# A new hand-written order for four engines, and fewer normalisation shifts, in a fused linear-attention and gated-MLP kernel

## The chip, the cores and the metric

The kernel runs on one core of one Trainium2 chip. The metric is the device time of one execution in microseconds (us), the median of several runs. The core has five engines that run independently and each take their instructions strictly in order: TensorE (PE, matrix products; the profile lists its weight loads apart as PEld), VectorE (DVE), ScalarE (ACT), GpSimd (POOL) and SyncE (SP, which only issues loads and stores here). An instruction that needs a result of another engine waits on a semaphore, and everything behind it on its own engine waits with it.

## The reference, cut to what matters

Inputs: q, k, v, alpha of shape (4 batches, 8 heads, 768 steps, 48), w_in (384 x 1024), w_spatial (768 x 768), b_spatial (768), w_out (512 x 384).

```
state = alpha[t][:, None] * state + k[t] (x) v[t]     # per batch and head, a 48 x 48 state
y[t]  = q[t] @ state                                   # 768 steps; heads joined: x is (4, 768, 384)
h = relu(x @ w_in); u, v = h[..., :512], h[..., 512:]
v_n = (v - mean(v)) / sqrt(var(v) + 1e-6)              # over the 512 columns of a row
v_s = w_spatial @ v_n + b_spatial                      # mixes the 768 rows of a batch
out = (u * v_s) @ w_out
```

## The kernel before

**The work and its tiles.** A batch has six chunks of 128 steps, so there are 24 chunks, numbered i = 0 to 23 (j = i // 2 numbers pairs of chunks). The recurrence is done by chunks: logarithms of alpha are summed by matmuls, exponentials of the sums scale k and q (`kt`, `qt`), both are turned by TensorE (`tr`, `trk`) and copied back (`ev`, `evs`), scores k by q are taken (`sc`) and multiplied by a mask (`m`, `ms`), and `y` adds masked scores times v and q times the state so far. Between chunks the state is carried: `upd` (k by v), `z` (sum with the old state), `S` (scaled by the decay), `sb` (bf16 copy). `xe` copies y out as the transposed input of the MLP. Chunks 0 to 3 and 6 to 9 are taken four at a time (`four_chunks`), 4 and 5 as a pair, the others singly.

The MLP follows per batch b: `v` and `u` (products with the two halves of w_in), `ve` and `ue` (relu out of the bank), then the normalisation of a row tile: `bn` (two VectorE instructions, L1068 and L1069: statistics), `rs` (two ScalarE instructions for a pair of row tiles, L1078 and L1079: 1 / sqrt(var + eps) as exp(-0.5 ln)), `nm` (the shift -mean / sqrt, L1085) and `vn`, the normalised tile. Then `s` (spatial mixing, for four column blocks d and two halves th of the rows; in two parts, of which the second needs the row tiles 4 and 5), `se` (bias added), `g` (times u), `o` (product with w_out), `oe` (copy out) and `st` (store).

**Two ways to normalise.** `vn` exists for two engines. ScalarE computes scale * x + shift and so needs `nm`; VectorE computes (x - mean) * rstd from the mean itself and never reads the shift. In the kernel before, one `nm` operation makes both shifts of a pair of row tiles, on VectorE, whichever engine normalises them: 12 operations, 24 instructions. Both `vn` of the pair depend on it.

```
def vnf(e, x=x):
    if e == "ACT":
        nc.scalar.activation(
            out=vn[n2][:, x, :], in_=v_sb[n2][:, x, :], func=AF.Identity, bias=shift[n2][:, x:x + 1],
            scale=rstd[n2][:, x:x + 1])
        return
    nc.vector.tensor_scalar(
        out=vn[n2][:, x, :], in0=v_sb[n2][:, x, :], scalar1=mvs[n2][:, x, 0:1],
        scalar2=rstd[n2][:, x:x + 1], op0=ALU.subtract, op1=ALU.mult)
```

**What sets the order.** Functions such as `pair`, `project_v`, `mix` only list operations, each with a key, the engines that could do it, what it depends on and how many of the eight PSUM banks it takes. The order, the engine of each operation and its banks stand in the string `PLAN`, which `replay` (L110) walks through: `D79` is operation 79 on VectorE (P TensorE, A ScalarE, G GpSimd, S SyncE), `@4,5` are its banks. Each engine gets its operations in the order of the table. `:512#0` puts a filler ahead of the operation: a matmul of the constant tile `junk` with 512 columns in fp32 into bank 0 (L243), whose result nobody reads; one filler is two matmul instructions in the profile. Before, there are seven fillers: three of 512 columns ahead of the first matmul, 512 and 424 ahead of the first state update `upd`, one of 192 and one of 376 ahead of two operations behind it.

**Loads.** SyncE issues all loads of q, k, v, alpha and the weights in one fixed order. Weights arrive as fp32 in two raw buffers in turn and are cast to bf16 (`cast`): w_in's v half, w_in's u half, three thirds of w_spatial, w_out. A raw buffer is loaded again only when all casts out of it are done; so the second third of w_spatial waits for the three casts of w_in's u half, and the last third for the two casts of the first third. w_spatial is turned in six steps on TensorE (`wt`) and copied back (`we`).

**Orders that matter below** (key.batch-or-chunk.index). VectorE between the last `qt` of chunks 4 and 5 and the last `vn` of batch 0, before: ev.k.2, ev.q.2, bn.0.2, bn.0.0, four m.2, bn.0.3, z.4, bn.0.1, nm.0.2, we.1, we.0, nm.0.0, ve.0.4, we.0, we.2, vn.0.0, vn.0.1, we.2, vn.0.3, bn.0.4, bn.0.5, two qt (chunks 6 to 9), nm.0.4, ue.0.2, vn.0.4; ScalarE normalises vn.0.2 and vn.0.5. GpSimd casts all three tiles of w_in's u half, then two vb, S.3, sb.3, both casts of w_spatial's first third, S.4. Around chunk 10 VectorE does bn.1.0, the first masks of chunks 10 and 11, z.10, their second masks, bn.1.1, bn.1.2, ve.1.3, bn.1.3.

Of the kernel before, what the change touches and what calls it, by code (L numbers as in the profile page):

```python
# [37 lines left out]
LETTERS = {"P": "PE", "D": "DVE", "A": "ACT", "G": "POOL", "S": "SP"}  # L38
# [4 lines left out]
D2 D0 D4 D1 G9 G11 G5 G6 D3 S56 S57 S59 S58 A60 S12 S169 S170 A61 S272 S171 D8 P62@0:512#0:512#0:512#0 P66@1 P67 P63  # L43
P70@2 P71 P74@3 P75 A68 A64 D79 G82 P91@4,5 P52@6 A69 A72 A76 G7 A78 A92 A84 A65 G88 G87 A73 A77 D85 D90 D81 D93 D53
D83 D80 P103@6,4,5,7:512#7:424#7 P94@0,1 D86 D104 D89 D106 G13 P97@6,2:192#2 D98 A95 P100@3,0 D101 A96 P117@3,6:376#1
P115@4,1 A99 G107 G14 A15 A173 D102 D109 P128@0,2 D119 D118 P174@5 A116 A122 A176 P130@6,4 S16 D132 D131 S172 A135
P175@1 A129 P120@3 P54@2 G110 G105 P136@0,4 A121 A178 A55 G111 G108 P133@6 G181 A180 A134 G184 A179 D112 A177 D138
P123@7,3 P141@2 S20 G276 G277 G278 G17 G19 G18 D124 D125 P151@6 P187@7,4 P126@3 S23 S274 S273 D185 A152 A127 G186 G183
G113 G114 D182 P190@5,6 A189 A192 A142 P144@3 D137 P139@4 D188 D191 A140 G22 G21 D153 D143 P199@6,5 P196@2,7 P162@4
A280 A145 P287@0 A163 P154@1 P160@3 A279 A288 A155 D200 D201 D198 D197 D164 P193@4 A161 P156@7 A157 A165 D194 D146  # L50
P158@5 A159 G195 P202@1,2 P203 S26 A204 A147 D166 P290@4 P37@5,7 D38 P34@3,6 G24 S275 S384 S396 G25 S503 S29 D35
P207@1 D148 D208 D36 A39 A289 P205 P281@7 P40@3,5 A206 A282 A167 G10 D42 P210@2 D149 D150 D41 S385 S386 D168 D209 S398
S397 P284@5 P223@6 P219@3 P221@1 A211 A291 A224 A285 D212 A283 A220 A213 D295 D301 A286 A292 D214 D222 D215 A216
P225@6 P233@2 P217@3 P229@7 P237@0 A218 A28 D298 G297 G27 D304 G294 P226 D227 G300 G303 P43@3,5 D45 P230 P234 D231
D235 A293 A44 P46@4,6 P306@5,1 D308 P238 P49@7,3 D50 D51 A48 A47 A307 P309@2,6 P315@1,4 P312@5,7 P249@3 P250 A310 A316
# [52 lines left out]


def replay(ops, held, warm, plan):  # L110

    for word in plan.split():
        word, *junk = word.split(":")
        word, *banks = word.split("@")
        op, eng = ops[int(word[1:])], LETTERS[word[0]]
# [1160 lines left out]
```

## Time and profile before

| | |
|---|---|
| median of 3 runs | 138.26 us (138.02 to 138.45) |
| the profiled execution | 139.19 us |
| its span, first to last instruction | 137.4 us |
| granted TensorE clock | 1.00 |
| instructions | 5308 |
| read from HBM, written | 23.60 MB, 4.72 MB |

The profile is of one execution. Its span lies 1.8 us below that execution's time; the rest is start and end of the program. A line of the timeline holds the start and length in us, the engine, the line of the kernel, the operation, what it writes from what, its shape and how many neighbours are merged; behind it in brackets the idle time ahead of it and what ended that. A line of the groups ends with busy us, mean ns of one, and the idle time before. In the chain of waits each piece is what held up the end of the program at that time. In the lines of stretches the busy time of each engine stands with its number of instructions. Lines L181, L185, L187 and L190 are helpers (copy, relu on ScalarE, relu on VectorE, product), L1006 every long matmul: there the tile names tell what it is.

### The profile page before, as it was taken

The page shows a single profiled execution, that of the slowest core. Times are in us where ns is not written, and L with a number is a line of the kernel's source. Part 1 is how long each engine was busy: PE and PEld are TensorE (multiplying, and loading weights), DVE is VectorE, ACT ScalarE, POOL GpSimd, SP SyncE. Part 2 cuts the span into 40 slices and gives each one's busy share as a digit, 9 for nine tenths or more (in the row PEclk, how much of TensorE's full clock was granted, in tenths as well). Part 3 has the DMA queues.
Part 4 walks back from the last instruction along what each step waited for, and adds up shares of the span by engine and source line. Part 5 has one row for each costly group of instructions (what it writes and reads, how often), then busy time and mean ns, then how long its engine had stood idle before and what let it go on. Part 6 is the DMA issues. An engine that isn't in the chain of part 4 may idle for free.

```text
span 137.4 us, 5308 instructions
## 1 busy us (share of the span) xinstructions
PE 131.0 (95%) x2122; PEld 79.2 (58%) x2122; DVE 120.8 (88%) x300; ACT 108.0 (79%) x261; POOL 87.2 (63%) x146
## 2 busy tenths in 40 slices
PE   6899998999999999999999999999999999999990
PEld 3365554564646566566657666656566765565560
DVE  6259999979999999999899999997999999974871
ACT  3476998899989889999997989999965796954041
POOL 7365899967399789972079989620799842003560
PEclk9999999999999999999999999999999999999999
DMA  3999999599989796899999797899991497101055
GB/s 83 371 371 382 341 321 347 132 374 383 366 164 261 159 218 127 163 184 192 195 190 209 143 205 147 167 194 226 190 181 23 158 390 257 66 0 57 0 203 203
DMA packets 76473, 28.66 MB, mean 209 GB/s; under 512 B 63008, under 2 KB 74912, under 8 KB 76448
## 3 DMA queue, kind: packets, MB, share of 16 engines
q1 hardware_dynamic: 76416, 28.32, 78.6%
q8 instruction: 16, 0.26, 0.8%
q14 instruction: 9, 0.07, 0.2%
q0 software_dynamic: 32, 0.00, 0.0%
HBM read 23.60 MB, written 4.72 MB: 206 GB/s over the span
## 4 chain that ended last, share of the span: by engine, by line
PE 76%; ACT 6%; DVE 6%; DMA 5%; issue 3%; POOL 2%; SPq 0%; POOLq 0%; ACTq 0%
PE bank L1006 53%; DMA kc<-in_k_dram 5%; PE bank L961 3%; PE bank L945 3%; PE bank L989 3%; PE bank L417 2%; PE bank L855 2%; PE bank L899 2%; PE bank L837 2%; PE bank L933 2%; DVE vn L1097 1%; PE bank L795 1%; PE bank L772 1%; ACT uT L185 1%; DVE w_spT L181 1%
## 5 line engine op out<-in xcount | busy, mean ns | idle before, releaser
L1006 PE MATMUL bank<-w_spT,vn 128*128 128x384 bf16 x192 | 35.8, 327 | 0.3 <-DVE vn L1097 0.3
L190 POOL TENSOR_TENSOR gT<-vs,uT 128x384 bf16<-128x384 f32 x28 | 25.7, 933 | 14.3 <-DVE vs L1153 14.1
L190 POOL TENSOR_TENSOR kt<-kc,binv 128x384 bf16<-128x384 f32 x22 | 20.3, 931 | 20.3 <-ACT binv L909 15.2
L1006 PEld LDWEIGHTS <-vn 128*128 128x128 bf16 x192 | 17.4, 98 | 11.7 <-DVE vn L1097 0.7
L1006 PE MATMUL bank<-w_in,xT 128*128 128x512 bf16 x72 | 19.1, 380 | 0.2 <-ACT xT L179 0.2
L1006 PE MATMUL bank<-xT,w_in 128*128 128x384 bf16 x96 | 18.7, 326 | 0.0
L1006 PE MATMUL bank<-w_out_sb,gT 128*128 128x384 bf16 (+1 forms) x100 | 18.4, 320 | 0.0
L1153 DVE TENSOR_TENSOR vs<-bank,bsp_bc 128x384 f32<-128x384 f32 x31 | 16.3, 550 | 2.4 <-PE bank L1006 2.3
L950 DVE TENSOR_TENSOR ptm<-bank,mask 128x512 bf16<-128x512 f32 x28 | 17.9, 683 | 0.4 <-PE bank L945 0.2
L179 ACT COPY kqT<-bank 128x512 bf16<-128x512 bf16 (+1 forms) x20 | 15.0, 792 | 3.1 <-PE bank L989 1.9
L1068 DVE BATCH_NORM_STATS2 stats<-v_sb 128x6 f32<-128x512 bf16 x24 | 16.4, 682 | 0.2
L185 ACT ACTIVATE v_sb<-bank 128x512 bf16<-128x512 f32 x20 | 11.8, 599 | 1.8 <-PE bank L1006 1.5
L185 ACT ACTIVATE uT<-bank 128x384 bf16<-128x384 f32 x27 | 12.4, 495 | 0.7 <-PE bank L1006 0.6
L1006 PEld LDWEIGHTS <-w_in 128*128 128x128 bf16 x96 | 9.0, 98 | 6.7 <-DVE ptm L950 0.3
L190 DVE TENSOR_TENSOR qt<-qc,bank 128x384 bf16<-128x384 f32 x24 | 12.6, 545 | 0.2 <-DMA qc<-in_q_dram 0.2
L1006 PEld LDWEIGHTS <-gT 128*128 128x128 bf16 x100 | 9.3, 98 | 5.8
L179 ACT CAST xT<-bank 128x384 bf16<-128x384 f32 x23 | 10.4, 482 | 1.8 <-PE bank L417 1.4
L844 DVE TENSOR_TENSOR ptm<-bank,mask 128x512 bf16<-128x512 f32 x16 | 10.4, 684 | 0.0
L1006 PEld LDWEIGHTS <-xT 128*128 128x128 bf16 x72 | 6.2, 97 | 6.2 <-ACT xT L179 1.2
L179 ACT COPY raw_w<-bank 128x384 f32<-128x384 f32 x8 | 3.8, 480 | 7.3 <-PE bank L1006 7.2
L394 DVE TENSOR_TENSOR zs<-bank,state 128x384 f32<-128x384 f32 x16 | 8.8, 549 | 0.5 <-PE bank L933 0.4
L243 PE MATMUL bank<-junk 128*128 128x512 f32 (+3 forms) x14 | 8.0, 700 | 1.1 <-DVE junk L1242 1.1
(162 smaller groups left out, 265.4 us busy)
## 6 DMA issues: line engine op xcount, KB each, us to landing
ac<-in_alpha_dram SPq DMA_DIRECT2D x14, 192.0 KB, 4.4
kc<-in_k_dram SPq DMA_DIRECT2D x14, 192.0 KB, 4.0
qc<-in_q_dram SPq DMA_DIRECT2D x14, 192.0 KB, 4.4
vc<-in_v_dram SPq DMA_DIRECT2D x14, 192.0 KB, 4.1
raw_w<-in_moe_w_spatial_dram SPq DMA_DIRECT2D x3, 768.0 KB, 8.0
out_dram<-o_sb SPq DMA_DIRECT2D x9, 192.0 KB, 2.0
ac<-in_alpha_dram SPq DMA_DIRECT2D x2, 768.0 KB, 6.8
kc<-in_k_dram SPq DMA_DIRECT2D x2, 768.0 KB, 7.6
```

What stands on the lines that cost most here:

```text
L179: nc.scalar.copy(out=out, in_=in_)
L185: nc.scalar.activation(out=out, in_=in_, func=AF.Relu)
L190: ENG[eng].tensor_tensor(out=out, in0=in0, in1=in1, op=ALU.mult)
L243: nc.tensor.matmul(out=banks[n][:, 0:cols].rearrange("p (a b) -> p a b", a=4), lhsT=junk, rhs=junk[:, None, 0:cols // 4].to_broadcast([128 ...
L394: lambda _: nc.vector.tensor_tensor(out=zs[i % 3], in0=tp(), in1=state[(i - 1) % 3], op=ALU.add),
L844: nc.vector.tensor_tensor(out=ptm[n2][:, ci, s], in0=banks[sl.bank].rearrange("p (hp t) -> p hp t", hp=HP), in1=mask[:, 3][:, None, :].to_ ...
L945: nc.tensor.matmul(out=pt[s][:, hp, :], lhsT=kT[rows, hp, :], rhs=qT[rows, hp, :], start=True, stop=True)
L950: nc.vector.tensor_tensor(out=ptm[n2][:, ci, s], in0=banks[sl_p[s].bank].rearrange("p (hp t) -> p hp t", hp=HP), in1=mask[:, 2][:, None, : ...
L961: nc.tensor.matmul(out=place(to, 3 * hp + (0, 1, 1, 2)[x]), lhsT=heads(vb, hp, x), rhs=ptm[n2][:, ci, x // 2, hp, :], start=(turn == 0), s ...
L1006: nc.tensor.matmul(out=ps, lhsT=lhsT, rhs=rhs, start=first and n == 0, stop=last and n == len(pairs) - 1)
L1068: nc.vector.bn_stats(out=stats[tt % 2], in_=v_sb[n2][:, tt, :])
L1153: nc.vector.tensor_tensor(out=vs[d], in0=banks[sl.bank][:, 0:TH], in1=bsp_bc[:, th, :], op=ALU.add)
```

## The change

The plan has a new text for all engines but SyncE: SyncE's 96 operations keep their order, key by key. `nm` becomes one operation per row tile, and emits its shift only if the table gives the `vn` of that tile to ScalarE. As an operation has to know its `vn`'s engine before that is emitted, `replay` first notes every engine. With 12 more `nm` the later operations have higher numbers.

```diff
 PLAN = """
-D2 D0 D4 D1 G9 G11 G5 G6 D3 S56 S57 S59 S58 A60 S12 S169 S170 A61 S272 S171 D8 P62@0:512#0:512#0:512#0 P66@1 P67 P63
...
+S56 D3 S57 D4 G9 S59 D0 D2 G11 D1 G5 S58 G6 D8 A60 S12 A61 P70@0:512#0:512#0:392#0 P66@1 P62@2 P67 P63 A68 P71 S171
...
 def replay(ops, held, warm, plan):
 
+    for word in plan.split():
+        op = ops[int(re.match("[A-Z]([0-9]+)", word).group(1))]
+        op.eng = LETTERS[word[0]]
     for word in plan.split():
...
-        def nm(_):
-            for x in (tt - 1, tt):
+        for x in (tt - 1, tt):
+            def nm(_, x=x):
+                if made[("vn", b, x)].eng == "DVE":
+                    return
                 nc.vector.tensor_scalar(
                     out=shift[n2][:, x:x + 1], in0=mvs[n2][:, x, 0:1], scalar1=rstd[n2][:, x:x + 1], scalar2=-1.0,
                     op0=ALU.mult, op1=ALU.mult)
 
-        op(("nm", b, tt - 1), "DVE", nm, [("rs", b, tt - 1), ("vn", b - 2, tt - 1), ("vn", b - 2, tt)])
-        for x in (tt - 1, tt):
+            op(("nm", b, x), "DVE", nm, [("rs", b, tt - 1), ("vn", b - 2, x)])
+
             def vnf(e, x=x):
...
             op(("vn", b, x), "DVE ACT", vnf,
-               [("rs", b, tt - 1), ("nm", b, tt - 1)] + [("s", b - 2, d, th, 1) for d in range(NDS) for th in range(2)])
+               [("rs", b, tt - 1), ("nm", b, x)] + [("s", b - 2, d, th, 1) for d in range(NDS) for th in range(2)])
```

What the new table holds, read by its keys:

| | before | new |
|---|---|---|
| `vn` on VectorE, on ScalarE | 18, 6 | 21, 3 |
| shift instructions | 24 | 3 |
| operations on VectorE without `nm` | 223 | 228 |
| operations on ScalarE, GpSimd | 234, 111 | 227, 113 |
| casts of weights on VectorE, ScalarE, GpSimd | 0, 4, 12 | 3, 2, 11 |
| fillers | 512, 512, 512; 512, 424; 192; 376 | 512, 512, 392; 512, 184 |

The sets of the first 88 TensorE operations are equal, and so are those of the last five.

VectorE in the stretch told above, new: ev.k.2, z.3, ev.q.2, a cast of w_in's u half, bn.0.0, four m.2, z.4, bn.0.1, bn.0.3, bn.0.2, we.0, vn.0.0, vn.0.1, we.0, vn.0.2, we.1, bn.0.4, vn.0.3, we.2, bn.0.5, we.3, ue.0.3, vn.0.4, vn.0.5; z.3 stood ahead of this stretch before. The other two casts of w_in's u half are on ScalarE and GpSimd. GpSimd then does S.3, sb.3, two vb, one cast of w_spatial's first third, S.4, and the other cast. Around chunk 10 VectorE has bn.1.0, one mask of chunk 10, the two of chunk 11, bn.1.1, bn.1.2, z.10, bn.1.3, sb.9, and then the other mask of chunk 10. TensorE has two output tiles and two u tiles of batch 1 more ahead of y.10. At the end of the last batch TensorE's order is: the last mixing result, three output tiles, and then the output tile that needs that result; VectorE does its `se`, the `g` that reads a bank, the `g` of that result; the last copy of an output is on ScalarE instead of VectorE.

More of the change, by code (lines that the diff above doesn't have):

```diff
@@ L42 @@
 PLAN = """
[L43 to L52, printed above, removed]
@@ L83 @@
[L83 to L87 removed]
+S56 D3 S57 D4 G9 S59 D0 D2 G11 D1 G5 S58 G6 D8 A60 S12 A61 P70@0:512#0:512#0:392#0 P66@1 P62@2 P67 P63 A68 P71 S171
```

80 lines of the change are left out of this document (45 added, 35 removed).

## The prediction

> **What bounds the kernel now.** I read the page first: the busy times, then the chain of work that ended last by engine.
>
> ```profile
> PE 131.0 (95%) x2122; PEld 79.2 (58%) x2122; DVE 120.8 (88%) x300; ACT 108.0 (79%) x261; POOL 87.2 (63%) x146
> ```
>
> ```profile
> PE 76%; ACT 6%; DVE 6%; DMA 5%; issue 3%; POOL 2%; SPq 0%; POOLq 0%; ACTq 0%
> ```
>
> TensorE carries three quarters of the chain, VectorE and ScalarE 6% each. A share hides where; so I asked for the busy time by stretch: after the length stand TensorE, its weight loads, VectorE, ScalarE and GpSimd, with their instructions, then the granted clock, the busy share of the DMA engines and GB/s.
>
> ```profile
> 12.00:28.00 16.00, 14.82 (x370) 8.71 (x362) 15.73 (x32) 13.66 (x32) 13.78 (x21) 1.00 0.98 298
> 28.00:38.50 10.50, 10.20 (x173) 5.72 (x171) 9.50 (x29) 10.20 (x28) 6.23 (x12) 1.00 1.05 360
> 50.00:120.00 70.00, 69.95 (x1154) 44.11 (x1153) 67.47 (x154) 61.87 (x156) 44.62 (x59) 1.00 0.82 182
> ```
>
> From 50 to 120 us TensorE idles 0.05 us in 70; there only fewer matmuls would help, and the change takes none away. Before 38.5 it is otherwise: from 12 to 28 VectorE is busy 15.73 of 16 us, TensorE lacks 1.18. The chain in order of time agrees: up to 38.5 us it ends in VectorE, after that it runs through TensorE to the end of its last matmul.
>
> ```profile
> 36.85 0.25 DVE shift L1085 x2
> 37.09 0.46 DVE uT L187
> 37.56 0.94 DVE vn L1097
> 38.54 0.50 PE bank L1006 x2
> ```
>
> A pair of shifts stands on that chain. So the time is: when VectorE has the six normalised tiles (`vn`) of batch 0 ready, plus a TensorE list that then runs almost without a gap.
>
> **The change part by part: the front.** VectorE from the landing of the first q to the last `vn` of batch 0:
>
> ```profile
> 11.69 1.48 DVE L190 TENSOR_TENSOR qt<-qc,bank 128x384 bf16<-128x384 f32 x3 [0.20 <-DMA qc<-in_q_dram]
> ...
> 29.65 0.34 DVE L1085 TENSOR_SCALAR shift<-mvs,rstd 128x1 f32<-128x1 f32 x2
> 30.68 0.62 DVE L181 COPY w_spT<-bank 128x384 bf16<-128x384 bf16 x2 [0.70 <-ACT rstd L1078]
> 31.22 0.33 DVE L1085 TENSOR_SCALAR shift<-mvs,rstd 128x1 f32<-128x1 f32 x2
> 31.55 0.69 DVE L187 TENSOR_SCALAR v_sb<-bank 128x512 bf16<-128x512 f32 x1
> ...
> 35.84 1.00 DVE L190 TENSOR_TENSOR qt<-qc,bank 128x384 bf16<-128x384 f32 x2
> 36.76 0.33 DVE L1085 TENSOR_SCALAR shift<-mvs,rstd 128x1 f32<-128x1 f32 x2
> 37.01 0.55 DVE L187 TENSOR_SCALAR uT<-bank 128x384 bf16<-128x384 f32 x1
> 37.47 1.01 DVE L1097 TENSOR_SCALAR vn<-v_sb,mvs,rstd 128x512 bf16<-128x512 bf16 x1
> ```
>
> The start, 11.69, is the landing of a load in a queue that keeps its order, so it stays. In the new table the same VectorE work lies between it and the last `vn`, but for this. Gone: three pairs of shifts (0.34, 0.33, 0.33), one eviction of v (0.69, to ScalarE) and one pair of `qt` (1.00, now behind the `vn`): 2.69. Added: two `vn` that ScalarE had and one cast of w_in that GpSimd had. Their prices:
>
> ```profile
> L1097 DVE TENSOR_SCALAR vn<-v_sb,mvs,rstd 128x512 bf16<-128x512 bf16 x18 | 7.6, 443 | 0.0
> L181 DVE CAST o_sb<-vc 128x384 bf16<-128x384 f32 x2 | 0.8, 443 | 0.0
> ```
>
> Two `vn` are 0.89. A cast of w_in on VectorE stands nowhere in this trace; 443 ns times 512/384 is 0.59 (an estimate from the cast of `vc`), which I take; the ends are 0.44 and 1.0, the second with a wait like that of the `vn` at 37.47. Swaps of equal kind (a `ue` for a `ue`, two `we` for two, one copy of a turned tile for another) cost nothing. Sum: 2.69 - 0.89 - 0.59 = 1.21 us less: the last `vn` ends at 38.48 - 1.21 = 37.3. The idle 0.70 before 30.68 and the 0.57 by which one `vn` at 37.47 exceeds the mean go or stay; both gone make 36.0. I take 0.4 of this 1.3: 36.9, a **lead of 1.6 us**, with ends 1.2 and 2.5.
>
> What is late next? The load of w_spatial, whose last third TensorE must turn before it can mix the second half of the rows. What it waits for:
>
> ```profile
> 23.31 1.73 POOL L181 CAST w_in<-raw_w 128x512 bf16<-128x512 f32 x3
> ```
>
> The second third of w_spatial loads only when all three casts of w_in end, at 25.04 on GpSimd alone. Now one each goes to VectorE, ScalarE and GpSimd, so they end near 23.31 + 0.58 = 23.9 and the queue behind them starts 1.1 us sooner. So this load gives about what VectorE gives.
>
> **From there to chunk 10.** The first 88 TensorE operations of both tables are the same set, so a lead carries on if nothing runs short. VectorE may: in the new table the masks of chunk 10 (`ms` 10) come behind three more statistics of batch 1. Now the four masks of chunks 10 and 11 end at 58.09, and TensorE uses them right behind its row of 58.34, from about 58.7:
>
> ```profile
> 54.18 0.68 DVE L1068 BATCH_NORM_STATS2 stats<-v_sb 128x6 f32<-128x512 bf16 x1
> 54.90 0.18 DVE L1069 BATCH_NORM_AGGREGATE mvs<-stats 128x2 f32<-128x6 f32 x1
> ```
>
> ```profile
> 56.81 1.28 DVE L950 TENSOR_TENSOR ptm<-bank,mask 128x512 bf16<-128x512 f32 x2
> ```
>
> ```profile
> 57.20 0.65 PE L1006 MATMUL bank<-xT,w_in 128*128 128x384 bf16 x3
> 57.69 0.81 PE L1006 MATMUL bank<-w_out_sb,gT 128*128 128x384 bf16 x4
> 58.34 0.33 PE L899 MATMUL bank<-la,le_one 128*128 128x384 bf16 x1
> ```
>
> VectorE's list up to there gains three statistics (3 x 0.86 = 2.58), the two `vn` (0.89), three casts (0.59 and twice 0.44) and a small copy (about 0.3), and loses the shifts (1.0), the eviction (0.69) and one state product (about 0.55): +3.0 by durations; back to back, instructions start about 0.08 before the last one ends, so +2.4. The masks end at 58.09 + 2.4 = 60.5 if VectorE regains no wait, at 59.2 if it regains the 1.3 from above; 59.7 in the middle. TensorE has four more operations ahead of this point (two output tiles, two u tiles; from one start to the next they take 58.34 - 57.69 = 0.65 and 57.69 - 57.20 = 0.49, so 2.3), so without a lead it would come at 61.0. So of the lead **1.2 us** is left here; the ends are 0.5 and 1.8.
>
> Behind it VectorE has room. Over the whole table 21 of 24 shifts go:
>
> ```profile
> L1085 DVE TENSOR_SCALAR shift<-mvs,rstd 128x1 f32<-128x1 f32 x24 | 3.9, 206 | 1.0 <-ACT rstd L1079 1.0
> ```
>
> 21 x 0.206 = 4.33 us off; three `vn` (1.33) and three casts (1.47) on; the rest swaps, with one operation fewer. Net 1.5 less at least, and 67.47 of 70 us leaves 2.5 idle. ScalarE gives three `vn` away. The fillers fall from seven to five where TensorE waits for loads or kt: nothing, as long as the clock holds (rival 2).
>
> **The tail** is dealt out anew:
>
> ```profile
> 129.53 1.02 DVE L1153 TENSOR_TENSOR vs<-bank,bsp_bc 128x384 f32<-128x384 f32 x2
> 130.58 1.10 DVE L190 TENSOR_TENSOR gT<-vs,uT 128x384 bf16<-128x384 f32 x1
> 131.60 0.56 DVE L190 TENSOR_TENSOR gT<-bank,uT 128x384 bf16<-128x384 f32 x1
> ```
>
> In the new table three output tiles (3 x 0.65 = 1.95 us) stand on TensorE between the last mixing result and the tile that needs it; VectorE has in that time an addition (0.55), a product from a bank (0.56) and a product of 0.56 to 1.10: 1.7 to 2.2. Stall 0 to 0.3; I take 0.3, with the last copy, now on ScalarE, in it.
>
> **Sum:** 1.2 - 0.3 = 0.9 us. The profiled execution took 139.19 (span 137.4 and 1.8 around it), so 138.3 for it; it lies 0.93 above the median of the runs, 138.26, which becomes 137.36, say **137.3**.
>
> **The rivals.** (1) *VectorE keeps TensorE waiting at chunk 10 (slower).* It decides from masks that end after 61.0 - 0.3 = 60.7: no wait of the front regained (60.5), and one of the added operations paying what the `vn` at 37.47 paid (0.57), gives 61.1; two give 61.6. Time: 138.26 + 0.6 = **138.9**. For it: both long cases, 1.01 at 37.47 and 1.10 at 130.58, ran beside GpSimd. The Trainium skill ("SBUF — State Buffer", Who interferes with whom) speaks of a lock, held for a whole instruction, between GpSimd and VectorE's copies, casts and tensor_scalar operations in a two-port mode. By that rule each of the added `vn` and casts risks such a wait, and each dropped shift stops risking one. (2) *The clock falls.* The fillers' weight loads show two rates:
>
> ```profile
> 2.92 0.34 PEld L243 LDWEIGHTS bank<-junk 128*128 128x128 f32 x1 [0.52 <-issue]
> 3.77 0.34 PEld L243 LDWEIGHTS bank<-junk 128*128 128x128 f32 x1 [0.52 <-issue]
> ```
>
> ```profile
> 10.59 0.19 PEld L243 LDWEIGHTS bank<-junk 128*128 128x128 f32 x1 [0.24 <-issue]
> 11.02 0.19 PEld L243 LDWEIGHTS bank<-junk 128*128 128x128 f32 x1 [0.24 <-issue]
> ```
>
> They follow one another after 0.85 us, later after 0.43, though the granted clock stands at 1.00: half rate for some 3 us. The new table has no filler between the first state update and the first scores. Another 3 us at half rate would lose 1.5: 137.3 + 1.5 = **138.8**. The Trainium skill ("TensorE: Matmul & The Clock Gate", Part 1) says that an idle window of about 3.4 us brings half rate back. The two spacings agree with its two rates; no gap of that length is in this trace. I find none in the new order either, where turns and small matmuls follow within a microsecond: a small chance. (3) *A load waits behind S.4.* GpSimd's new order puts the state product S.4 ahead of the second cast of w_spatial's first third, and behind that cast waits the load of its last third, and with it SyncE's queue:
>
> ```profile
> 27.25 1.60 POOL L181 CAST w_row<-raw_w 128x768 bf16<-128x768 f32 x2
> 29.00 0.83 POOL L190 TENSOR_TENSOR sbd<-zs,bc 128x384 bf16<-128x384 f32 x1
> ```
>
> ```profile
> 28.88 2.42 SPq L1048 DMA_DIRECT2D raw_w<-in_moe_w_spatial_dram  x1
> ```
>
> If VectorE's sum for S.4 comes no sooner than now (by 29.00), S.4 (0.83) and one cast (0.80) stand between it and the load, which issues at 30.6, some 1.7 us late, and takes the lead with it: **138.2**, no change. Against it: the DMA engines are full from 28 to 38.5 (1.05), so a late issue eats a backlog first. (4) *All waits go:* 1.8 and no stall in the tail, and more where loads come sooner: 2.4, **135.9**.
>
> **How the numbers follow.** A measurement of this kernel tells about 0.3% (0.4 us) from no change. Forecast, 136.5 to 137.8: 0.48. Rival 4: 0.12. Rival 1: 0.17. Rival 2: 0.07. Rival 3: 0.16, of which 0.01 slower. Faster 0.48 + 0.12 = 0.60, within 0.15, slower 0.17 + 0.07 + 0.01 = 0.25. The range, 135.8 to 139.1, reaches to rival 4 and past rival 1 by half of a second wait.
>
> **What would show it.** Three shifts in the group; the first mixing matmul that needs the last `vn` near 36.9 instead of 38.54; the load of the last third of w_spatial by 28.9; chunk 10's masks near 59.7; TensorE's last matmul near 133.3; matmuls of 15 to 25 us at their old spacing. I am wrong if TensorE idles for over 1 us in one place behind 50 us, or if that load issues after 30.

## The result and the profile after

The changed kernel takes 143.15 us, the median of 4 runs (142.37 to 143.74), against 138.14 for the kernel before beside it (137.86 to 138.45): ratio 1.036, 95% interval 1.029 to 1.043. It is 5.0 us slower, and the range ended at 139.1. The profiled execution took 143.67 us, with a span of 141.9. The ratios in this document leave out runs that lie over 1.5% above the fastest of their kernel, which the medians keep.

The page of the changed kernel: busy times, the granted clock in 40 slices of 3.5 us, the DMA engines' busy share, and the chain by engine.

```profile
PE 132.8 (94%) x2118; PEld 79.3 (56%) x2118; DVE 123.0 (87%) x284; ACT 105.6 (74%) x254; POOL 88.5 (62%) x148
PEclk9999658999999999999999999999999999999999
DMA  3999999199999976989799789989920179320064
PE 71%; DVE 11%; DMA 8%; ACT 3%; SPq 2%; issue 2%; ACTq 0%; DVEq 0%
```

Three things are new. VectorE has 16 instructions fewer and is busy 2.2 us longer; its share of the chain goes from 6% to 11%. The clock is down in three slices between 14 and 25 us. And the DMA engines idle in the slice from 25 to 28 us. The stretches of the front have the same columns as before the prediction:

```profile
12.00:16.00 4.00, 3.34 (x125) 2.22 (x124) 3.86 (x9) 2.68 (x8) 3.17 (x8) 0.91 1.13 349
16.00:20.00 4.00, 3.95 (x64) 2.38 (x58) 3.68 (x7) 2.78 (x7) 3.46 (x6) 0.50 1.06 328
20.00:24.00 4.00, 4.00 (x94) 2.27 (x98) 2.86 (x6) 3.05 (x9) 3.26 (x4) 0.74 1.05 359
24.00:28.00 4.00, 3.88 (x90) 2.32 (x91) 3.96 (x9) 3.98 (x9) 3.94 (x7) 1.00 0.25 74
```

VectorE, which worked 15.73 of these 16 us before, now works 14.36: it waits. Its timeline shows for what, and what the normalisation of batch 0 costs:

```profile
12.13 1.02 DVE L194 TENSOR_TENSOR qt<-qc,bank 128x384 bf16<-128x384 f32 x2 [0.17 <-DMA qc<-in_q_dram]
20.55 1.89 DVE L848 TENSOR_TENSOR ptm<-bank,mask 128x512 bf16<-128x512 f32 x3 [0.50 <-PE bank L841]
23.54 0.55 DVE L194 TENSOR_TENSOR qt<-qc,bank 128x384 bf16<-128x384 f32 x1 [0.64 <-ACT bank L503]
25.21 1.03 DVE L185 CAST w_in<-raw_w 128x512 bf16<-128x512 f32 x1
32.69 1.73 DVE L1103 TENSOR_SCALAR vn<-v_sb,mvs,rstd 128x512 bf16<-128x512 bf16 x2
34.60 0.40 DVE L1103 TENSOR_SCALAR vn<-v_sb,mvs,rstd 128x512 bf16<-128x512 bf16 x1
36.00 0.38 DVE L1103 TENSOR_SCALAR vn<-v_sb,mvs,rstd 128x512 bf16<-128x512 bf16 x1
38.09 1.94 DVE L1103 TENSOR_SCALAR vn<-v_sb,mvs,rstd 128x512 bf16<-128x512 bf16 x2
```

The last vn of batch 0 ends at 38.09 + 1.94 = 40.03, where the prediction had 36.9. Four of six vn take about 0.9 to 1.0 us, the other two 0.4. GpSimd's timeline beside them:

```profile
25.13 0.83 POOL L194 TENSOR_TENSOR state<-zs,bcq 128x384 f32<-128x384 f32 x1
30.04 0.83 POOL L194 TENSOR_TENSOR sbd<-zs,bc 128x384 bf16<-128x384 f32 x1 [1.76 <-ACT binv L745]
32.62 1.65 POOL L185 CAST w_row<-raw_w 128x768 bf16<-128x768 f32 x2
37.18 2.70 POOL L194 TENSOR_TENSOR kt<-kc,binv 128x384 bf16<-128x384 f32 x3 [2.91 <-ACT binv L745]
```

Compare ends. The two casts on GpSimd end at 32.62 + 1.65 = 34.27, the vn beside them at 32.69 + 1.73 = 34.42; the three kt at 39.88, the vn at 40.03: both 0.15 later. VectorE's cast of w_in ends at 26.24, the state product beside it at 25.96. So each of these VectorE instructions finishes only when a GpSimd instruction has ended. The row at 30.04 is S.4, ahead of the second cast of w_spatial's first third; the loads behind those casts:

```profile
18.39 8.37 SPq L1052 DMA_DIRECT2D raw_w<-in_moe_w_spatial_dram  x2
31.67 0.37 SPq L1052 DMA_DIRECT2D raw_w<-in_moe_w_spatial_dram  x1
```

The last third is loaded from 31.67, not by 28.9. TensorE then waits in three places ahead of 44 us, 1.5 us together, and again at 67 and 136:

```profile
35.32 0.32 PE L713 MATMUL bank<-la,lt_quad 128*128 128x384 bf16 x1 [0.69 <-DVE w_spT L185]
40.09 0.66 PE L1010 MATMUL bank<-w_spT,vn 128*128 128x384 bf16 x3 [0.58 <-DVE vn L1103]
41.01 0.81 PE L1010 MATMUL bank<-w_spT,vn 128*128 128x384 bf16 x4 [0.26 <-DVE qt L194]
67.23 0.34 PE L903 MATMUL bank<-la,le_one 128*128 128x384 bf16 x1 [0.50 <-DVE qt L194]
136.16 2.13 PE L1010 MATMUL bank<-w_out_sb,gT 128*128 128x384 bf16 x16 [0.25 <-DVE gT L194]
```

### The profile page after: what moved, and what is told of

Its sections match the earlier page's. It is cut to its first block, busy times and chain, and to the rows that moved or that the text cites. A ratio compares the mean times of both kernels' runs of the same rounds, so it can differ in the third digit from the quotient of the medians.

```text
span 141.9 us, 5277 instructions
## 1 busy us (share of the span) xinstructions
PE 132.8 (94%) x2118; PEld 79.3 (56%) x2118; DVE 123.0 (87%) x284; ACT 105.6 (74%) x254; POOL 88.5 (62%) x148
## 4 chain that ended last, share of the span: by engine, by line
PE 71%; DVE 11%; DMA 8%; ACT 3%; SPq 2%; issue 2%; ACTq 0%; DVEq 0%
PE bank L1010 47%; DMA qc<-in_q_dram 6%; DVE vn L1103 3%; PE bank L993 3%; PE bank L949 3%; PE bank L841 2%; PE bank L965 2%; DMA ac<-in_alpha_dram 2%; PE bank L421 2%; SPq L675 2%; PE bank L903 2%; PE bank L859 2%; DVE qt L194 2%; PE bank L937 1%; DVE kqT L185 1%
## 5 line engine op out<-in xcount | busy, mean ns | idle before, releaser
L1010 PE MATMUL bank<-w_spT,vn 128*128 128x384 bf16 x192 | 36.3, 326 | 0.9 <-DVE vn L1103 0.6
L194 POOL TENSOR_TENSOR gT<-vs,uT 128x384 bf16<-128x384 f32 x29 | 26.4, 929 | 16.3 <-DVE vs L1159 15.4
L1010 PE MATMUL bank<-xT,w_in 128*128 128x384 bf16 x96 | 19.8, 326 | 0.3
L183 ACT COPY kqT<-bank 128x512 bf16<-128x512 bf16 (+1 forms) x20 | 15.6, 809 | 3.5 <-PE bank L776 1.5
L189 ACT ACTIVATE uT<-bank 128x384 bf16<-128x384 f32 x24 | 11.4, 491 | 7.2 <-PE bank L1010 6.9
L189 ACT ACTIVATE v_sb<-bank 128x512 bf16<-128x512 f32 x21 | 12.3, 598 | 1.6 <-PE bank L1010 1.3
L183 ACT CAST xT<-bank 128x384 bf16<-128x384 f32 x20 | 9.1, 489 | 3.5 <-PE bank L421 1.7
L1103 DVE TENSOR_SCALAR vn<-v_sb,mvs,rstd 128x512 bf16<-128x512 bf16 x21 | 11.0, 547 | 0.3 <-ACT rstd L1083 0.3
L185 POOL CAST sbd<-state 128x384 bf16<-128x384 f32 x12 | 6.1, 510 | 6.2 <-DVE state L194 5.9
```

Of the source, the lines that this page charges most:

```text
L183: nc.scalar.copy(out=out, in_=in_)
L185: ENG[eng].tensor_copy(out=out, in_=in_)
L189: nc.scalar.activation(out=out, in_=in_, func=AF.Relu)
L194: ENG[eng].tensor_tensor(out=out, in0=in0, in1=in1, op=ALU.mult)
L1010: nc.tensor.matmul(out=ps, lhsT=lhsT, rhs=rhs, start=first and n == 0, stop=last and n == len(pairs) - 1)
L1103: nc.vector.tensor_scalar(out=vn[n2][:, x, :], in0=v_sb[n2][:, x, :], scalar1=mvs[n2][:, x, 0:1], scalar2=rstd[n2][:, x:x + 1], op0=ALU.su ...
```

## The experiments

A landmark serves below: the first turn of chunk 3's k, TensorE's 66th operation. There all engines have done the same operations in both tables, loads apart. (Some expectations give 41.0 us for it, the end of the operation behind it.) TensorE's rows, first before, then after:

```profile
40.20 0.40 PE L772 MATMUL bank<-ident,kt 64*128 64x64 bf16 x16
```

```profile
42.88 0.40 PE L776 MATMUL bank<-ident,kt 64*128 64x64 bf16 x16
```

So 2.7 of the profile's 4.5 us are lost by then. A landmark is of one execution, and it scatters: e1, e2, e8 and f2 have the same order up to it and stand at 39.69, 39.66, 39.89 and 39.04; the changed kernel and e3 share theirs and stand at 42.88 and 41.59 (mean clocks 0.975 and 0.986). Two landmarks that differ by less than about 0.9 us therefore show no difference by themselves. All runs, with the ratio to the kernel before on the same chip:

| run | median us | ratio (95% interval) | landmark |
|---|---|---|---|
| changed kernel | 143.15 | 1.036 (1.029 to 1.043) | 42.88 |
| e1 old table, shifts dropped | 138.56 | 1.002 (0.999 to 1.005) | 39.69 |
| e2 old to the 88th, then new | 141.31 | 1.024 (1.019 to 1.029) | 39.66 |
| e3 new to the 88th, then old | 145.01 | 1.051 (1.044 to 1.058) | 41.59 |
| e4 new, old fillers | 143.27 | 1.036 (1.033 to 1.039) | 42.61 |
| e5 e4, casts on ScalarE | 142.90 | 1.031 (1.025 to 1.036) | 42.12 |
| e6 e5, vn.0.5 on ScalarE | 143.34 | 1.033 (1.028 to 1.039) | 42.48 |
| e7 e4, sums and casts early | 143.30 | 1.033 (1.027 to 1.039) | 41.95 |
| e8 old, new tail | 142.71 | 1.026 (1.020 to 1.032) | 39.89 |
| e9 old order, new engines | 161.29 | 1.167 (1.159 to 1.175) | 43.79 |
| e10 new order, old engines | 153.57 | 1.109 (1.103 to 1.115) | 44.03 |
| e11 front mended | 143.66 | 1.039 (1.033 to 1.044) | 43.51 |
| e12 old, new fillers | 140.50 | 1.007 (1.003 to 1.010) | 38.98 |
| f1 new to the landmark, then old | 141.86 | 1.023 (1.018 to 1.028) | 42.56 |
| f2 old to the landmark, then new | 140.89 | 1.016 (1.012 to 1.021) | 39.04 |
| f3 new to the 41st, then old | 140.98 | 1.019 (1.014 to 1.024) | 41.56 |
| f4 new from the 41st to the landmark | 139.94 | 1.010 (1.006 to 1.015) | 40.57 |
| g1 f4, one cast early | 140.11 | 1.012 (1.008 to 1.016) | 40.50 |
| g2 e4, front mended again | 142.98 | 1.032 (1.027 to 1.038) | 41.66 |

The theory at the start (A): the loss is in the new table, most of it ahead of 50 us, by late loads and by vn that wait for GpSimd. Rivals: the clock; the order behind; the shifts' rule itself.

### The shifts alone (e1)

```diff
 PLAN = """
-(the new table)
+(the table of before; each nm of a pair of tiles as two nm of one tile)
```

> The table of before with the new rule for shifts: of 24 shift instructions 6 stay, those of the six tiles that ScalarE normalises. Everything else is as before. Theory A (the loss is all in the table; the dropped shifts are worth what the prediction said of them, 0.17 us each where VectorE sets the end): of the six shifts of batch 0 four go, 0.7 us off the chain up to the last vn of batch 0, and about as much is left at the end: 137.4 to 137.8 us against 138.1. Rival B (VectorE has slack around the shifts, or what it gives back another wait takes): 138.1, no change.

Measured: no change. VectorE works less, 118.5 us against 120.8; the landmark stands 0.5 us earlier, which is within the scatter. In the trace one normalisation no longer waits:

```profile
37.31 0.40 DVE L1103 TENSOR_SCALAR vn<-v_sb,mvs,rstd 128x512 bf16<-128x512 bf16 x1
37.42 0.97 POOL L185 CAST w_row<-raw_w 128x768 bf16<-128x768 f32 x1 [0.88 <-DMA raw_w<-in_moe_w_spatial_dram]
```

This vn took 1.01 before, when it began 0.04 us ahead of GpSimd's cast. Here it begins 0.11 ahead, takes 0.40, and the cast takes 0.97 instead of 0.82: now GpSimd waits. But no time that can be told from no change comes of it. Rival B holds: the dropped shifts are worth nothing that these runs can tell, and the loss is all in the table.

### Front or rest (e2, e3, e8, f1, f2)

The two tables are joined at a TensorE operation: up to it all engines follow one, behind it the other.

```diff
 PLAN = """
-(the new table)
+(old table up to TensorE's 88th operation; then what is left, in the order of the new)      e2
+(new up to the 88th; then old, banks dealt out anew)                                        e3
+(old up to the 226th; then new)                                                             e8
+(new, old fillers, up to the 66th; then old)                                                f1
+(old up to the 66th; then new)                                                              f2
```

> The table of before for all engines up to TensorE's 88th operation (cums.11, which ended at 49.7 us before and at 52.2 in the changed kernel), then the new table from there on; the shifts by the new rule. In the profiles the changed kernel is 2.4 us late at this point and 4.1 at the end. Theory A (most of the loss is made in the front, and what is lost behind it is the new order's own): 138.1 plus 1.0 to 1.7, so 139.1 to 139.8. Rival B (the losses behind the front only follow from a late start of loads and buffers there): 138.0, no change. Rival C (the rest is the whole loss, the front would be made good): 141 or more.

> The mirror image: the new table up to TensorE's 88th operation, then the order of before; the PSUM banks behind this point are dealt out anew, to the bank that has been free longest. Theory A: the front's loss alone, 138.1 plus 2.4, so 140.5 (139.5 if the clock stays up). Rival B (all the loss comes from the front): 143. Rival C (the front is made good): 138.5.

> The table of before with the new rule for shifts (138.56 us in its run) up to TensorE's 226th operation of 265 (o.2.5, which ended at 114 us), and the new table for all engines behind it. Theory A (the tail alone costs: a product that waits for GpSimd, 1.17 instead of 0.55 us, 0.3 us of TensorE waiting, the last copy on ScalarE 0.3 us later): 139.1 to 139.4. Rival B (the new tail only looks worse, because the order ahead of it hands VectorE's work over late): 138.3 to 138.6.

The first three don't settle it, though by time e2 reaches its theory C and e3 passes its rival B, which can't both be. At the seam of e2 TensorE waits 0.5 us for a copy of ScalarE, as the tables had not done the same work there; e8 has 2.0 us of such a wait in one place (`<-DVE ptm`, the masks of chunks 22 and 23, which the old table had not made by then); e3 loses more at several places behind the seam, where its banks are others than in either table, and its clock was at 0.971 to 0.988, so that its 145.0 says little of the front. Hence the cut at the landmark.

> The new table with the old fillers up to TensorE's 66th operation (ends at 41.0 us before), where all engines have done the same operations in both tables; then the order of before. Theory A (the front's loss of 2.2 us, as the profile of the kernel with the old fillers has it at this point, stays to the end): 138.3 + 2.2 = 140.5. Rival B (the old order makes good what was late): 139.3 or less. Rival C (as in e3, a late front makes the old order late by as much again): 142 or more.

> The order of before up to the same point, then the new table. Theory A (the rest has a loss of its own: 0.5 us at 65 us where VectorE is behind, 0.65 us by the neighbours that TensorE's operations have, 0.3 in the tail and 0.3 for the last copy): 138.3 + 1.8 = 140.1, and e2's 3.0 held 0.5 us of its seam. Rival B (no loss but where the seam was): 138.5 or less. If the losses add, f1 and f2 together make the 5.0 us.

The front alone costs 2.3% (3.3 us), the rest alone 1.6% (2.4 us); together 1.023 x 1.016 = 1.040, within the interval of the changed kernel. By time f1 lies between its theories A (2.2 us) and C (3.7 or more), and f2 is past its theory A (1.8 us). TensorE's landmark and last rows in f1, then in f2:

```profile
42.56 0.40 PE L776 MATMUL bank<-ident,kt 64*128 64x64 bf16 x16
133.73 2.77 PE L1010 MATMUL bank<-w_out_sb,gT 128*128 128x384 bf16 x20
```

```profile
39.04 0.40 PE L776 MATMUL bank<-ident,kt 64*128 64x64 bf16 x16
63.95 0.34 PE L903 MATMUL bank<-la,le_one 128*128 128x384 bf16 x1 [0.50 <-DVE qt L194]
132.87 2.13 PE L1010 MATMUL bank<-w_out_sb,gT 128*128 128x384 bf16 x16 [0.26 <-DVE gT L194]
```

From the landmark to the end of TensorE's last matmul f1 needs 133.73 + 2.77 - 42.56 = 93.94 us. The other traces with the old order behind the landmark (before, e1, e12, f3, f4, g1) need 93.9 to 94.0 as well, whether their landmark stands at 38.98 or at 41.56. So a late front stays late, as A has it, and neither B nor C holds.

With the new table on both sides of the landmark (changed kernel, e4, e5, e7, e11, g2) the same stretch takes 95.4 us in all six; e6, with one more wait, takes 95.8. So the new order behind the landmark loses 1.5 us of its own. Of these 0.50 and 0.25 are the two waits at 67 and 136 us. About 0.7 stands in no wait: the operations are the same, only their neighbours differ. f2 needs 135.00 - 39.04 = 95.96, 0.5 more than those six, of which 0.26 is a wait at 39.7 right behind its cut; its 2.4 us are therefore too much for the rest. In the two profiles the last matmul ends at 138.29 and 134.18; the 4.1 us between them are the 2.68 at the landmark and 1.44 behind it.

Both waits stand behind VectorE instructions that end with GpSimd's. In the changed kernel VectorE has no gap from 63.97 us to the two qt for which TensorE waits:

```profile
63.97 1.32 DVE L1103 TENSOR_SCALAR vn<-v_sb,mvs,rstd 128x512 bf16<-128x512 bf16 x2
65.68 0.57 DVE L1103 TENSOR_SCALAR vn<-v_sb,mvs,rstd 128x512 bf16<-128x512 bf16 x1
66.17 1.00 DVE L194 TENSOR_TENSOR qt<-qc,bank 128x384 bf16<-128x384 f32 x2
```

The second of the two vn merged in the first row takes 1.00, and the one at 65.68 takes 0.57; they end 0.15 and 0.14 behind an instruction of GpSimd. That is 0.77 above two vn of 0.40, more than the wait of 0.50. The product ahead of the wait at 136 is told in the last section. That the waits go when GpSimd's work is moved was not run.

### The clock (e4, e12)

```diff
-P103@5,4,6,7:512#7:184#7 ... P97@3,1 ... P117@0,1
+P103@5,4,6,7:512#7:424#7 ... P97@3,1:192#1 ... P117@0,1:376#1     e4: upd.0, tr.k.1, sc.0
```

> The new table with the fillers between 11 and 16 us that the table of before had: 512 and 424 columns ahead of the first state update (new: 512 and 184), 192 ahead of the turn of the second k, 376 ahead of the first scores (new: none). The three fillers ahead of the first matmul stay as in the new table. Theory A (the half-rate matmuls of 14 to 22 us come from the missing fillers; runs of the changed kernel whose mean granted clock was 1.00 were 1.2 us shorter than those of 0.975): granted clock 1.00 in every run and 141.7 to 142.5 against 143.15 for the changed kernel. Rival B (the slow clock makes everything late: the casts, the load of w_spatial, the vn): 139.5 or less. Rival C (fillers delay the scores by their own length, some 0.7 us, and the clock falls anyway): 143.5.

```diff
-P103@6,4,5,7:512#7:424#7 ... P97@6,2:192#2 ... P117@3,6:376#1
+P103@6,4,5,7:512#7:184#7 ... P97@6,2 ... P117@3,6                 e12: upd.0, tr.k.1, sc.0; ahead of the first matmul 392 for a 512
```

> The table of before with the new rule for shifts (138.56 us), and the fillers of the new table: 512, 512, 392 columns ahead of the first matmul, 512 and 184 ahead of the first state update, none behind. Theory A (the fillers keep the clock up, and without them the matmuls of 14 to 22 us run at half rate): granted clock below 1.00 in some runs, the matmuls of the projections at 20 us 0.81 instead of 0.41 us longer than their half, and 0.5 to 1.5 us lost, 139 to 140. Rival B (the fillers are dispensable, and without the 192 and 376 columns in the way the first scores come 0.3 us sooner): 138.0 to 138.6, clock 1.00.

e4 is as slow as the changed kernel, with a clock of 0.996 or more in every run and the same waits (0.7 at a copy of w_spatial, 0.6 at the vn, 0.5 at 67 us); the two runs of the changed kernel whose clock was 1.00 took 142.37 and 142.64. So the slow clock is real but not the main cause: it goes with the 1.2 us by which the changed kernel's other two runs (0.975 and 0.976, both about 143.7) are longer. In e4 the clock came as in theory A and the time as in C, 0.8 us above the changed kernel's runs at 1.00; whether the fillers' own length is that 0.8 was not tested. In e12 five of ten runs showed a clock of 0.964 to 0.976 and took 141.3 to 142.9; the other five, at 1.00, took 138.3 to 139.8. So theory A's clock came in half the runs, at some 3 us, a higher price than it said. The five runs at 1.00 are 0.7% slower than before (e1: 0.2%), and the two intervals touch: whether the old table needs its fillers apart from the clock stays open. None of the 56 runs of the kernel before fell below 0.996. The old fillers alone don't keep the clock up in other orders: f3 and g2 have them, and each had a run at 0.971 and 0.964 (141.92 and 145.75 us).

### Mending the front (e5, e6, e7, e11, g2)

```diff
-G24 ... G25 ... D219
+A24 ... A25 ... D219          e5: casts of w_spatial's second third
+A24 ... A25 ... A219          e6: and vn.0.5
-P120 G111 P177 ... D17 G19 ... G197 ... G22
+P177 P120 G111 ... G19 G17 ... G22 G197      e7: cum.2.1, y.0; casts of w_in; S.4
+(e5 and e7, D86 ahead of D104, P100 ahead of P128)      e11: qt.1.0, S.0; tr.q.1, pm.2
+(e5 and e7, A27 ahead of A296)                          g2: cast of the last third, ebc.3
```

> The kernel with the old fillers (143.27 us), but both casts of w_spatial's second third are on ScalarE instead of GpSimd, at the same places of the table. In that kernel GpSimd makes them from 32.4 to 34.0 us, and vn.0.0 and vn.0.1 on VectorE beside them take 0.90 and 0.91 instead of 0.40; TensorE then waits 0.7 for a copy of w_spatial that VectorE makes right behind. Theory A (a GpSimd instruction that is running when a vn starts holds it until it ends): both vn take 0.40, VectorE is 1.0 us further, the 0.7 us wait at 35 us goes; vn.0.4 and vn.0.5, beside the kt of GpSimd, stay at 1.0 each unless they come ahead of the first kt: 142.3 to 142.7. Rival B (the vn are slow for another reason, or ScalarE is late by the 1.5 us of the casts and the copies behind it keep TensorE waiting): 143.3 or more.

> As the kernel before it in this list, and the last normalisation of batch 0 (vn.0.5) on ScalarE, as it was before the change; its shift is emitted again. In the kernel with the old fillers vn.0.4 ends at 38.85 and vn.0.5, which waits for a kt, at 39.77. Theory A: vn.0.5 runs on ScalarE beside vn.0.4, the mixing that needs both starts 0.7 to 0.9 us sooner, 141.5 to 142.0. Rival B (TensorE at 39 to 43 us waits for the exponentials and turned k and q, which ScalarE then delivers 0.8 us later): as the kernel without this, 142.3 to 143.3.

> The kernel with the old fillers (143.27 us), with three moves back towards the order of before: the second sum of chunk 4's logarithms on TensorE ahead of y.0 (the new table has it behind, where it ends 2.1 us later than before; the exponentials, GpSimd's kt and the casts behind it wait for it); all three casts of w_in's u half off VectorE (two on GpSimd, one on ScalarE); S.4 on GpSimd behind the second cast of w_spatial's first third, whose load of the last third waits for it. Nothing is changed at the vn. Theory A (late loads are part of the loss): the casts of w_in end near 25 us instead of 26, the DMA engines idle less from 24 to 28 us, the last third of w_spatial is loaded by 29.5, and about 1 us is gained: 142.0 to 142.6. Rival B (up to 40 us VectorE sets the end, and loads have slack): only the cast's 1.0 us of VectorE counts, and the waits for GpSimd beside the vn shift: 142.3 to 143.3. The two differ in where the gain stands: in A TensorE is ahead from 22 us on, in B only from 35.

VectorE's vn and GpSimd beside them in e5:

```profile
32.34 0.73 DVE L1103 TENSOR_SCALAR vn<-v_sb,mvs,rstd 128x512 bf16<-128x512 bf16 x2
37.95 1.33 DVE L1103 TENSOR_SCALAR vn<-v_sb,mvs,rstd 128x512 bf16<-128x512 bf16 x2 [0.42 <-ACT rstd L1083]
37.19 2.85 POOL L194 TENSOR_TENSOR kt<-kc,binv 128x384 bf16<-128x384 f32 x3 [4.87 <-ACT binv L745]
```

With the casts away from GpSimd the two vn at 32 us take 0.73 together, not 1.73. That shows the wait: nothing else was changed at them. It gives VectorE 1.0 us; the 0.42 in brackets is VectorE waiting where it had not. e7 loads the last third from 29.31 instead of 31.4. At the landmark e5 is 0.5 us earlier than e4, e6 0.1 and e7 0.7, all within the scatter, and no median of the three can be told from e4's. That these causes lie side by side, so that each covers the next, would explain it, but is not shown.

> The kernel with the old fillers (143.27 us) with all the front's mends at once: casts of w_spatial's second third on ScalarE; chunk 4's second sum ahead of y.0; the casts of w_in's u half off VectorE; S.4 behind the cast; and new, the last q of chunk 1 (qt.1.0) on VectorE ahead of S.0 and its turn on TensorE ahead of a product of the mask, as the order of before had it, so that the scores of chunk 0 come 0.5 us sooner or more. In the profiles the single mends brought 0.4 us (casts, e5) and 0.7 us (scores and casts, e7) at TensorE's 65th operation, of the 2.4 us that the new front is late there. Theory A (these causes stand one behind the other, so that the gains add): 1.1 to 2.0 us earlier there than with the old fillers alone, 141.3 to 142.2. Rival B (they lie side by side, each covers the other): no more than e7's 0.7 us earlier, 142.6 to 143.3.

Neither theory: e11 is 0.9 us later at the landmark than e4, and 143.66 us in time. TensorE's rows:

```profile
16.42 0.35 PE L819 MATMUL bank<-o_sb,ident 32*32 32x384 bf16 x7 [0.59 <-ACT vb L183]
16.70 1.28 PE L247 MATMUL bank<-junk 128*128 128x376 f32 x2
17.91 0.61 PE L841 MATMUL bank<-kqT 48*128 48x128 bf16 x8
```

The product moved back, pm.2, holds a bank that the next one needs, and ScalarE empties it late; then a filler comes, in good part at half rate (1.28 us, 0.90 in e4). The first scores, which the move was to bring sooner, start at 17.91; in e4 at 16.92. The clock of this execution was 0.988; the three others, at 0.996 to 1.00, took 143.3 to 143.7, no less than e4.

> The kernel with the old fillers (143.27 us) with the mends of e5 (both casts of w_spatial's second third on ScalarE) and of e7 (chunk 4's second sum ahead of y.0, casts of w_in off VectorE, S.4 behind the cast), and the move of g1; without the move of qt.1.0 and its turn, behind which TensorE waited for a bank in e11. Theory A (the single gains at TensorE's 65th operation, 0.4 and 0.7 us, and up to 0.9 for the cast, add): 141.3 to 141.9. Rival B (what is gained at one is waited for at the next): 0.7 us at that point at most, 142.5 or more.

At the landmark it is 0.95 us earlier than e4 (41.66), between A and B and hardly above the scatter; in time 0.3 us, within the intervals, which is B's.

### Inside the front (f3, f4, g1)

```diff
+(new, old fillers, up to TensorE's 41st operation; then old)           f3
+(old; between the 41st and the 66th new; then old)                     f4
+(f4, A27 ahead of A296)                                                g1
```

> As f1, but the new table only up to TensorE's 41st operation (29.0 us before; the kernel with the old fillers is 0.9 us late there). Theory A (late scores of chunks 0 to 3 and late casts of w_in, before any vn, make half of the front's loss, and it stays): 139.2. Rival B (w_spatial's load and VectorE have slack behind this point, the 0.9 us is regained): 138.3 to 138.7.

> The order of before, and only between TensorE's 41st and 66th operations the new one (29 to 41 us: the stretch of the normalisation of batch 0 and the casts of w_spatial). Theory A (the vn that wait for GpSimd, and w_spatial's copies behind them, cost here by themselves; 1.3 us in the profile of the kernel with the old fillers): 139.6. Rival B (they only cost what they do because the front arrived late and met the casts): 138.3 to 138.7, and the vn in this stretch near 0.40 us.

> The kernel f4 (139.94 us: order of before, new only between TensorE's 41st and 66th operations) with one move: the cast of the first tile of w_spatial's last third on ScalarE ahead of the copy and the two exponentials of chunks 3 and 4 that wait for VectorE, instead of behind them. In f4 it stands at 39.49 to 40.33 us, though its load has landed near 37.5 and ScalarE idles from 37.38 to 38.23; TensorE waits for it. Nothing is changed at the vn, of which four still wait for GpSimd. Theory A (the cast's place is what costs): TensorE's turn of this third starts near 39.2 instead of 40.4, 0.9 us gained, 138.8 to 139.3. Rival B (the vn and the qt behind them set the end, the cast is only last by a little): no gain, 139.7 to 140.2.

Both halves lose. f3 loses 0.8 us up to its cut (late scores and casts, no vn yet) and 1.1 more just behind, where TensorE waits for an eviction on ScalarE that the old table had done by then: a seam, so f3's 2.5 us are too much for the first half. f4, with an old, punctual start, stands 0.7 to 1.5 us behind the four landmarks of the old order and loses in time (1.0%; e1: 0.2%), and four of its vn take 0.54 to 1.00, so the vn's waits need no late front. g1 moved the cast to 37.62 and gained nothing: its theory A falls. In g1 the chain of waits runs through VectorE:

```profile
36.39 1.39 DVE vn L1103 x2
37.78 0.94 DVE qt L194 x2
38.72 0.04 issue
38.76 1.62 PE bank L1010 x9
```

These two vn (0.40 each without a wait) stand ahead of the two qt whose bank TensorE needs at 38.76. How much of f4's loss is the vn's waits and how much TensorE's other order there stays open.

### Order and engines apart (e9, e10)

```diff
+(order, banks and fillers of before; each operation's letter from the new table)           e9
+(order and banks of the new table, old fillers; each operation's letter from the old)      e10
```

> The order of before (every operation at its old place, old banks, old fillers), but each operation on the engine that the new table gives it: 80 operations change engine, among them vn.0.2, vn.0.5 and three vn of batch 1, which go from ScalarE to VectorE, the casts of w_in, w_spatial and w_out, the copies xe, ve, oe. Three shifts stay. Against 138.56 us for the old table with the new rule for shifts. Theory A (the dealing out is the loss: VectorE gets work that waits for GpSimd where VectorE sets the end): 140.5 to 142. Rival B (the sequence on each engine is the loss, the engines matter little): 138.5 to 139.5. Operations whose engine was chosen for another place can stand badly here, so a loss between is to be read from the trace, not from the time alone.

> The mirror image: the order of the new table with the old fillers (143.27 us), but each operation on the engine that it had before; six shifts. Theory A (the dealing out is the loss): 139.5 to 141. Rival B (the sequence is the loss): 142.5 or more.

By the tables 90 operations change engine, not the expected 80. e9 misses both theories by 19 us. e10 lies above B's 142.5, but 10 us above the new table itself, which neither foresaw. An engine's order and what is given to it hold only together, so the question "order or engines" has no answer of this form.

## Why the prediction was wrong

**The failed step is the sum of the front.** It added durations, each at the mean of its kind, along a VectorE that was to lose no further time. What VectorE's instructions cost beside GpSimd, up to 0.6 us each, was left to rival 1. The same sum with what was measured, in stretches from the first qt to the last vn, before and after (VectorE is the third busy time):

```profile
11.69:38.48 26.79, 25.33 (x543) 14.58 (x542) 25.52 (x60) 24.15 (x58) 20.30 (x33) 1.00 1.01 324
```

```profile
12.13:40.03 27.90, 25.74 (x540) 14.85 (x535) 26.12 (x54) 22.42 (x55) 20.93 (x34) 0.88 0.95 310
```

- *The prices of the added vn and cast* were the mis-sized terms. The six vn rows of after add up to 1.73 + 0.40 + 0.38 + 1.94 = 4.45 us; those of before, quoted here, to 2.21, and with the 0.89 taken for two more to 3.10. That is 1.35 too little. The cast took 1.03, just above the upper end, not 0.59: 0.44. Busy time was to fall by 1.21 and rose by 26.12 - 25.52 = 0.60, a miss of 1.81, of which these two are 1.79.

```profile
32.94 0.73 DVE L1097 TENSOR_SCALAR vn<-v_sb,mvs,rstd 128x512 bf16<-128x512 bf16 x2
33.85 0.47 DVE L1097 TENSOR_SCALAR vn<-v_sb,mvs,rstd 128x512 bf16<-128x512 bf16 x1
37.47 1.01 DVE L1097 TENSOR_SCALAR vn<-v_sb,mvs,rstd 128x512 bf16<-128x512 bf16 x1
```

- *The idle time.* 0.4 of it and of the one long vn was to go; it grew from 1.27 to 1.78 (0.51): the new order has new waits, for scores and for exponentials. The load of q landed later, so the first qt began at 12.13 instead of 11.69 (0.44); in e4 and f1, with the new order too, it began at 11.86 and 11.82, so most of this belongs to the one execution. 1.81 + 0.51 + 0.4 + 0.44 = 3.16; the miss is 40.03 - 36.9 = 3.13.
- *The path.* The sum took VectorE for the path from 11.69 on. In the chain of waits of before, VectorE comes only from 30.69 on; it runs mostly through TensorE to 25 us and then through ScalarE. Late scores ahead of that were no term of the sum, and the casts were to come sooner; f3 has both late, and is 0.8 us behind at its cut.
- *Loads.* The casts of w_in were to end at 23.9 and ended at 26.24, as VectorE reached its own only then. Rival 3 happened too, by more than it said (31.67 against 30.6). An issue after 30 was the prediction's own sign of being wrong. e7, with that load at 29.31, is no faster in time: the load alone is not what keeps the front late.
- *Chunk 10.* Its masks were to end at 59.7 with 1.2 us left; they end at 63.58, and TensorE, late itself, comes at 63.65 (the rows of VectorE, then TensorE, behind this list). The wait on VectorE comes 3.6 us later, 0.50 at 67.23, behind two vn that waited for GpSimd; f2 has it with an old front as well. Rival 1 named this engine and this mechanism and priced it 0.6 us, once, at one place. It struck at five instructions ahead of 41 us, and at two more ahead of 67.
- *Behind the landmark* "VectorE has room" went by busy time alone and put the loss at nothing. The six traces show 1.5 us, about half of it in no wait.
- *The tail* was to cost 0.3, with the last copy in it. TensorE waits 0.25, and the last copy ends 0.41 us behind TensorE's last matmul, 0.40 before: this term held.
- *The shifts.* Their three pairs were 1.0 of the 2.7 us that were to go. e1 drops 18 shifts, four of them in batch 0, and gains nothing that can be told. The prediction also counted a dropped shift as a wait not risked; none of the 24 shifts of before took over 0.22 us.
- *The clock.* Rival 2 was held small as no long idle time was to be seen. The clock fell in two of four runs though TensorE's longest idle time between 7 and 16 us was 0.36. The Trainium skill ("TensorE: Matmul & The Clock Gate", Part 1) names an idle window of some 3.4 us for half rate, and in the same Part a kernel whose clock went up and down because TensorE was idle often and briefly. This trace shows half rate without a long gap, so the absence of one is no safety. Which short gaps matter no run here shows: in e12's trace TensorE was busy 2.49 of the 4 us from 12 to 16, the changed kernel's 3.34, and e12's clock stayed at 1.00.

```profile
62.90 0.68 DVE L954 TENSOR_TENSOR ptm<-bank,mask 128x512 bf16<-128x512 f32 x1
```

```profile
63.65 0.41 PE L965 MATMUL bank<-ptm,vb 128*32 128x128 bf16 x16
```

What held: that TensorE waits for VectorE's last vn at the end of the front (0.58 at 40.09), the three shifts, the tail, and that most is decided in the front. What stays open is how much of the front's 2.7 us each cause has: the waits for GpSimd are shown at the instructions, but no run shows the kernel's time without all of them. For GpSimd's hold on VectorE the Trainium skill ("SBUF — State Buffer", Who interferes with whom) gives the rule, an exclusive lock on a shared pair of ports for a whole instruction; the trace agrees, with the 0.15 us above. The prediction cited it and then summed with a mean over waiting and unhindered vn.

## What to carry to other kernels

When an order is dealt out anew, a mean duration is no price: split it into the unhindered one and the wait, and ask for every moved VectorE instruction that only touches SBUF what GpSimd does in that moment. A busy engine with slack on average gives no proof of slack in a list that other engines feed; if two tables have a point at which all engines have done the same operations, join them there, and the cost of each side can be measured. A single mend in such a front can be lost in the scatter: read a landmark in several traces of the same order first, to know how far it moves by itself.

## What the runs showed of the hardware

- A vn on VectorE (bf16, SBUF to SBUF) takes 0.38 to 0.41 us unhindered and otherwise ends 0.14 to 0.15 us after the GpSimd instruction that holds it. VectorE's cast of w_in ended 0.28 after (26.24 and 25.96). A product of two SBUF tiles waits as well: the last such g took 1.17 from 134.94 and ended 0.41 behind GpSimd's last g (131.85 + 3.85 = 135.70). A qt, which reads one operand from PSUM, kept its 0.54 us beside GpSimd's casts.
- Who holds whom turns on less than 0.1 us: a vn that began 0.04 ahead of a GpSimd cast waited (1.01, before), one that began 0.11 ahead did not (0.40, e1).
- TensorE's own list for the same operations can be longer by another order without an idle row: from the landmark to the last matmul, less the waits, by some 0.7 us of 94.
